# Top-k attention and MLP mixer on one core: score matmuls in chunks of 256 keys, PV over full rows, and a new order

## The chip, the cores and the metric

The kernel runs on one core of a Trainium2 chip. The metric is the device time of one execution in microseconds. The kernel before was timed three times: median 919.33 us, 917.88 to 922.02. The profile comes from one more execution (915.43 us), whose span from the first to the last instruction is 913.6 us.

## What is computed

The attention has 8 batches, 8 heads, 576 positions and a head size of 64; of each row of scores only the 32 largest take part. Its output feeds a mixer MLP over tokens and then over channels.

```python
scores = scale * np.matmul(q, k.transpose(0, 1, 3, 2))          # 8 x 8 x 576 x 576
kth = np.partition(scores, -32, axis=-1)[..., -32:-31]
scores = np.where(scores >= kth, scores, -1e9)
attn = softmax(scores)
x = matmul(attn, v) as [8, 576, 512]
h = relu(x.T @ w_tok1) @ w_tok2                                 # tokens: 576 -> 256 -> 576
u = x + h.T
out = u + relu(u @ w_ch1) @ w_ch2                               # channels: 512 -> 1536 -> 512
```

## The kernel before

**Tiling.** Two heads form a pair, and there are 32 pairs, four to a batch. Keys and queries of a pair are transposed on TensorE, so that head 0 lies on partitions 0 to 63 and head 1 on 64 to 127 of `qT` and `kT`. The 576 queries are cut into five groups `g` of 128; the fifth has 64 queries of each head, and both heads share one tile in it. So a pair has nine rows of work, called heads here: two for each of the groups 0 to 3, and one for group 4.

**A unit of work** is one group of a pair (`unit_ops`, line 419). TensorE computes the scores into PSUM tiles `big`, one for each head, in fp32, which takes two passes per matmul in the trace (`scores`, line 355; L367 for groups 0 to 3, L358 for group 4). ScalarE copies them to `S` (L424). VectorE finds the maxima in seven segments (L431), reduces them (L434, L435, L442) to a first threshold `thi`. ScalarE compares (L445), GpSimd, called POOL in the profile, builds `X` (L448), and VectorE takes from it the 32nd largest value `tlo` (L460). With that threshold the probabilities `Pm` are made in one of several forms:

- D: ScalarE takes the exponential, POOL builds a mask and multiplies (L470 to L479).
- R: ScalarE builds `M`, which is zero for a kept score (L486). TensorE computes the scores a second time and adds `M` times a large negative diagonal, `sink`, to them in PSUM (L504 to L509). ScalarE's exponential of the sum is zero where the sink went in (L512). Q is like R with POOL building `M`.
- A: ScalarE takes the exponential into PSUM, and VectorE compares and multiplies in one instruction (L520).

`FORMS` (line 25) gives the form of each group, one string for even pairs and one for odd ones.

**PV.** A DMA transposes `Pm` into `PT`, ten blocks of 128 x 128, five blocks of keys for each head. `Pm` has 640 columns, of which the last 64 are zeros, written once at the start. `pv` (line 383, matmuls at L390) then multiplies the blocks with `vb`, the values with a column of ones behind them, 65 columns. The fifth block holds only 64 keys, and the kernel before lets that matmul run on 64 rows (`kr`). A pair has 5 groups x 2 heads x 5 blocks = 50 matmuls. VectorE normalises (`norm`, L408 and L409) into `Xb`.

**MLP.** After four pairs of a batch, `mlp_ops` (line 549) runs the mixer: L574 and L579, L595 to L602, L617, L635 and L640 on TensorE, with ScalarE's evictions at L608, L623 and L648.

**The order.** Each piece of work is entered in a `Plan` (line 46) with its engine, an expected duration in us, a due time, what it depends on, and which buffers it takes and frees. `Plan.run` is a list scheduler: on each engine it takes the piece that can start first, and of nearly equal ones the one that is due first. The instructions are issued in the order that comes out, and each engine works through its own in that fixed order. The due times are `W` (line 19) times `T`. So the numbers in `plan.add(...)` and `W` decide no arithmetic, only the order. The four PSUM tiles `big`[...] are the scarcest buffers: scores, transposes, PV, the repeated scores, form A's exponential and the MLP all take theirs from them.

At the end VectorE checks counts and thresholds, and a branch (from line 852) recomputes everything exactly if the check fires; with these inputs it isn't taken.

Of the kernel before, what the change touches and what calls it, by code (L numbers as in the profile page):

```python
# [8 lines left out]
P = 128  # L9
# [7 lines left out]
SINK2 = float(2.0**50)  # L17

W = dict(
    T=2.75, ev=1.35, evh=0.6, seg=0.35, t2=1.2, ct=4.85, xm=3.0, dm=2.3, m5=3.05, ex=3.45, tn=2.3,  # L20
    z=5.1, mk=3.65, pm=4.55, rw=3.7, og=4.8, eg=4.5, ea=3.2, st=4.65, tr=1.7, pv=6.0, fin=6.85,
    mlp=8.85, stp=1.45,
)

FORMS = ("DRADD", "RDADR")
NEG = -float(2.0**120)
BIG = float(2.0**60)

# [143 lines left out]
def kernel(  # L172
# [19 lines left out]
    B, H, S, D = q.shape  # L192
# [6 lines left out]
    SM = 512  # L199
    ST = S - SM  # L200
# [15 lines left out]
    plan = Plan()  # L216
# [69 lines left out]
    T = W["T"]  # L286
# [8 lines left out]
    def pair_ops(p):  # L295
        b, h0 = divmod(p, 4)
        h0 *= 2
        t0 = 9 * p * T
        qL, kL, vL, vb = Buf("qL"), Buf("kL"), Buf("vL"), Buf("vb")
        qT, kT = Buf("qT"), Buf("kT")  # L300
        keng = nc.scalar if p == 0 else nc.sync

        def ld_main(buf, src, eng):
            for h in range(2):
                eng.dma_start(
                    out=buf.t[:, 0:4, h, :],
                    in_=src[b, h0 + h, 0:SM, :].rearrange("(p t) d -> p t d", t=4),
                )

        def ld_q():  # L310
            ld_main(qL, q, nc.sync)
            for h in range(2):
                nc.sync.dma_start(
                    out=qL.t[64 * h : 64 * h + ST, 4, h, :], in_=q[b, h0 + h, SM:S, :]
                )

        def ld_kv(buf, src, eng):
            def f():
                ld_main(buf, src, eng)
                eng.dma_start(  # L320
                    out=buf.t[0:ST, 4, :, :],
                    in_=src[b, h0 : h0 + 2, SM:S, :].rearrange("h p d -> p h d"),
                )
            return f

        tl = t0 - 12 * T
        lq = plan.add("SP", 0.24, tl, ld_q, acq=[qL], dma=1.4)
        lk = plan.add("SP", 0.2, tl + 0.1, ld_kv(kL, k, keng), acq=[kL], dma=1.4)
        lv = plan.add("SP", 0.2, tl + 0.2 if p else 4 * T, ld_kv(vL, v, nc.sync), acq=[vL], dma=1.4)

        pq, pk = Buf("big"), Buf("big")

        def tr(dst, src, n):
            def f():
                o = flat(dst.t)
                for t in range(n):
                    nc.tensor.transpose(o[:, t * P : (t + 1) * P], src.t[:, t, :, :], identF[:, :])
                if n == 4:
                    nc.tensor.transpose(o[:, SM:S], src.t[0:ST, 4, :, :], identF[0:ST, 0:ST])
            return f  # L340

        tt = t0 - W["tr"] * T
        oq = plan.add("PE", 0.6, tt, tr(pq, qL, 5), [lq], acq=[pq, qT], use=[qL])
        ok = plan.add("PE", 0.6, tt + 0.5 * T, tr(pk, kL, 4), [lk], acq=[pk, kT], use=[kL])

        def cp(dst, src, n):
            return lambda: nc.scalar.activation(  # L347
                out=dst.t[:, 0:n], in_=flat(src.t)[:, 0:n], func=AF.Copy, scale=HUP)

        eq = plan.add("ACT", 0.6, tt + T, cp(qT, pq, 5 * P), [oq], use=[pq, qT])  # L350
        ek = plan.add("ACT", 0.57, tt + 1.5 * T, cp(kT, pk, S), [ok], use=[pk, kT])
        ov = plan.add("ACT", 0.6, t0 + 4 * T, lambda: nc.scalar.copy(
            out=vb.t[:, :, :, 0:D], in_=vL.t[:, :, :, :]), [lv], acq=[vb], use=[vL])

        def scores(g, bs, stop):
            if g == 4:
                for lo, hi in ((0, SM), (SM, S)):
                    nc.tensor.matmul(  # L358
                        out=flat(bs[0].t)[:, lo:hi], lhsT=qT.t[:, SM : SM + P], rhs=kT.t[:, lo:hi],
                        start=True, stop=stop,  # L360
                    )
                return

            for lo, hi in ((0, SM), (SM, S)):
                for h in range(2):
                    r = slice(64 * h, 64 * h + 64)
                    nc.tensor.matmul(  # L367
                        out=flat(bs[h].t)[:, lo:hi], lhsT=qT.t[r, g * P : (g + 1) * P],
                        rhs=kT.t[r, lo:hi], start=True, stop=stop,
                    )  # L370

        PT = []
        for g in range(5):
            n = 2 if g < 4 else 1
            bs, Ss = [Buf("big") for _ in range(n)], Buf("S")
            i0 = 9 * p + 2 * g
            om = plan.add("PE", 1.05, T * i0, lambda g=g, bs=bs: scores(g, bs, True), [eq, ek], acq=bs + [Ss], use=[qT, kT])
            PT.append(unit_ops(i0, n, bs, Ss, om, p, g, scores, [qT, kT]))


        O, rd = Buf("big"), Buf("rd")

        def pv(gs):
            for g in gs:
                src = PT[g][0].t
                for h in range(2):
                    o = O.t[:, h, 0 : 5 * (D + 1)].rearrange("p (t d) -> p t d", t=5)
                    for j in range(5):
                        kr = P if j < 4 else ST
                        nc.tensor.matmul(  # L390
                            out=o[:, g, :], lhsT=src[0:kr, (5 * h if g < 4 else 0) + j, :],
                            rhs=vb.t[0:kr, j, h, :], start=(j == 0), stop=(j == 4),
                        )

        if b not in xb:
            xb[b] = Buf("Xb")
        X = xb[b]
        tv = t0 + (9 + W["pv"]) * T
        o = None
        for gs in ((range(5),) if p < NPAIR - 1 else ((0, 1), (2,), (3,), (4,))):  # L400
            o = plan.add("PE", 0.44 * len(gs), tv + gs[0], lambda gs=gs: pv(gs), [PT[g][1] for g in gs] + [ov, o],
                         acq=([] if o else [O] + ([X] if X.users == 0 else [])),
                         use=[PT[g][0] for g in gs] + [vb, X, O])


        def norm():
            o = O.t[:, :, 0 : 5 * (D + 1)].rearrange("p h (t d) -> p h t d", t=5)
            nc.vector.reciprocal(rd.t[:, :, :], o[:, :, :, D])  # L408
            nc.vector.tensor_tensor(  # L409
                out=X.t[:, :, h0 * D : (h0 + 2) * D].rearrange("p t (h d) -> p h t d", h=2),  # L410
                in0=o[:, :, :, 0:D], in1=rd.t[:, :, :].unsqueeze(3).to_broadcast([P, 2, 5, D]), op=ALU.mult,
            )

        nm = plan.add("DVE", 0.86, tv + T, norm, [o], acq=[rd], use=[O, X])
        mixed.setdefault(b, []).append(nm)
# [3 lines left out]
    def unit_ops(i0, n, s, S_, om, p, g, scores, qkT):  # L419

        sg, X, Pm, PT = Buf("sg"), Buf("X"), Buf("Pm"), Buf("PT")
# [60 lines left out]
        elif form in ("R", "Q"):  # L482
# [18 lines left out]
                    op1=ALU.max), zs, acq=[Wm], use=[Z])]  # L501

            def again():
                scores(g, es, False)  # L504
                for h in range(n):
                    for lo, hi in ((0, SM), (SM, S)):
                        nc.tensor.matmul(  # L507
                            out=flat(es[h].t)[:, lo:hi], lhsT=sink[:, "RQ".index(form), :], rhs=Wm.t[:, h, lo:hi],
                            start=False, stop=True)  # L509

            og = plan.add("PE", 1.05 + 0.25 * n, te + W["og"] * T, again, ws, acq=es, use=[Wm] + qkT)
            last = [plan.add("ACT", 0.535, te + W["eg"] * T + 0.2 * h, lambda h=h: nc.scalar.activation(  # L512
                out=Pm.t[:, h, 0:S], in_=flat(es[h].t)[:, 0:S], func=AF.Exp, scale=scale / UP),
                [og], acq=[Pm] if h == 0 else [], use=[es[h], Pm]) for h in range(n)]
# [34 lines left out]
    def mlp_ops(b):  # L549
        X = xb[b]  # L550
        fin = b == B - 1
# [59 lines left out]
        for fc in range(NF):  # L611
            pb = Buf("big")

            def f(fc=fc, pb=pb):
                for lo, hi in ((0, SM), (SM, S)):
                    for cc in range(NC):
                        nc.tensor.matmul(  # L617
                            out=flat(pb.t)[:, lo:hi], lhsT=wc1b[:, cc, fc * P : (fc + 1) * P],
                            rhs=UT.t[:, cc, lo:hi], start=(cc == 0), stop=(cc == NC - 1))

            d = due()
            o = plan.add("PE", 1.05, d, f, uts + l3, acq=[pb] + ([H2] if fc == 0 else []), use=[UT, H2])
            h2.append(plan.add("ACT", 0.535, d + 1, lambda fc=fc, pb=pb: nc.scalar.activation(  # L623
                out=H2.t[:, fc, :], in_=flat(pb.t)[:, 0:S], func=AF.Relu), [o], use=[pb, H2]))
        for s0 in (0, 2, 4):
# [4 lines left out]
            for h in range(sn):  # L630
                for part in range(2):
                    def f(part=part, sc=s0 + h, h=h, pb=pb, r=r):
# [5 lines left out]
                        if part:  # L638
                            for cc in range(NC):
# [2 lines left out]
                                    start=False, stop=(cc == NC - 1))  # L642

                    d = due()
                    o = plan.add("PE", 1.55 if part else 1.3, d, f, dep + l4,
                                 acq=[pb, ob] if (h, part) == (0, 0) else [], use=[H2, pb] + ([UT] if part else []))
                    dep = [o]
            e = plan.add("ACT", 0.1 + 0.4 * sn, d + 1, lambda pb=pb, ob=ob, r=r, sn=sn: nc.scalar.copy(  # L648
# [255 lines left out]
```

## Time and profile before

| | us or share |
|---|---|
| time, median of 3 | 919.33 |
| span of the profiled execution | 913.6 |
| TensorE busy (PE) | 809.9, 89% |
| VectorE busy (DVE) | 794.2, 87% |
| ScalarE busy (ACT) | 757.1, 83% |
| GpSimd busy (POOL) | 722.3, 79% |
| score matmuls L367, busy | 269.9 |
| PV matmuls L390, busy | 125.6 |
| mean granted TensorE clock | 0.885 |

Busy is the union of an engine's instructions in time, so matmuls that overlap count once. PEld is the loading of weights, which runs beside the matmuls. PEclk in a view is the share of full clock that the chip granted TensorE in that stretch: 1.00 is full speed and 0.50 half. In the lists of groups, a line gives the source line, the engine, the operation, output and inputs, the shapes and the count; then busy us and the mean ns of one, and behind the second bar the idle time ahead of the group with what ended it. In the list of waits, a line reads: who waited, for whom, us in total, times, the longest in us.

### The profile page before, as it was taken

To read this page: it belongs to the slowest core of one execution; us is meant where nothing else is said; L and a number is where in the kernel's file an instruction comes from. 1 tells how busy PE (TensorE), PEld (TensorE's weight loads), DVE (VectorE), ACT (ScalarE), POOL (GpSimd) and SP (SyncE) were. 2 spreads that over 40 slices of the span, in tenths; PEclk is the share of its full clock that TensorE was granted. 3 is DMA by queue.
4 is the path that set the end of the run, shared out by engine and by line. 5 is a ranking of instruction groups with operands and counts; after the bars stand their busy time and mean duration, and the time that the engine had idled before them with its cause. 6 is when DMAs were issued, how large, how long until landed. Compare 5 with 4: busy or idle time off the path is not lost.

```text
span 913.6 us, 19343 instructions
## 1 busy us (share of the span) xinstructions
PE 809.9 (89%) x5411; PEld 465.4 (51%) x5411; DVE 794.2 (87%) x4780; ACT 757.1 (83%) x1428; POOL 722.3 (79%) x557
## 2 busy tenths in 40 slices
PE   7778788989899989999789988899799998899996
PEld 4445544555555545555455554555455544455553
DVE  5988999989999999989998998899899889997630
ACT  6876979878999989979889888898898788996641
POOL 2888898879888989869878888888788798886800
PEclk9655769989899999989789997999899898997888
DMA  5965664454654555354544464544563535332501
GB/s 129 155 110 110 112 119 90 77 103 97 139 83 99 128 125 106 73 112 104 104 87 90 98 130 100 83 93 111 107 124 65 116 84 110 66 66 44 108 10 56
DMA packets 311028, 89.57 MB, mean 98 GB/s; under 512 B 303744, under 2 KB 305664, under 8 KB 310912
## 3 DMA queue, kind: packets, MB, share of 16 engines
q1 hardware_dynamic: 306960, 84.19, 45.8%
q0 software_dynamic: 2752, 3.77, 2.9%
q8 instruction: 44, 0.72, 0.3%
q14 instruction: 72, 0.59, 0.2%
q10 hardware_dynamic: 1200, 0.30, 0.1%
HBM read 35.85 MB, written 9.44 MB: 50 GB/s over the span
## 4 chain that ended last, share of the span: by engine, by line
PE 53%; DVE 24%; ACT 13%; POOL 4%; issue 3%; DMA 2%; SPq 1%; DVEq 0%; ACTq 0%; POOLq 0%
PE big L367 15%; PE big L390 12%; PE big L635 11%; DVE cd L431 9%; PE big L617 6%; DVE tlo L460 5%; ACT sg L445 4%; ACT S L424 3%; PE big L507 3%; DVE cd L435 3%; PE big L358 2%; DVE Pm L520 2%; ACT M L486 2%; DVE Xb L409 1%; DVE m L434 1%
## 5 line engine op out<-in xcount | busy, mean ns | idle before, releaser
L431 DVE MAX8 cd<-S 128x8 f32<-128x82 f32 (+1 forms) x2016 | 404.6, 231 | 23.6 <-ACT S L424 23.4
L448 POOL TENSOR_TENSOR X<-S,sg 128x1152 f32<-128x1152 f32 (+1 forms) x160 | 343.0, 2159 | 60.4 <-ACT sg L445 57.8
L367 PE MATMUL big<-kT,qT 64*128 64x512 f32 (+1 forms) x1288 | 269.9, 523 | 32.4 <-ACT kT L347 18.6
L445 ACT ACTIVATE sg<-S,thi 128x576 bf16<-128x576 f32 x288 | 225.6, 785 | 23.5 <-DVE thi L442 19.4
L367 PEld LDWEIGHTS big<-kT,qT 64*128 64x128 f32 x1288 | 149.1, 223 | 153.9 <-issue 95.4
L460 DVE MAX8 tlo<-X 128x8 f32<-128x588 f32 x288 | 220.5, 766 | 5.4 <-POOL X L448 4.8
L424 ACT COPY S<-big 128x576 f32<-128x576 f32 x288 | 175.0, 644 | 42.0 <-PE big L367 34.7
L479 POOL TENSOR_TENSOR Pm<-E,M 128x1152 bf16<-128x1152 bf16 (+1 forms) x79 | 169.6, 2147 | 6.3
L390 PE MATMUL big<-vb,PT 128*128 128x65 bf16 (+1 forms) x1600 | 125.6, 205 | 8.7 <-ACT H L623 4.0
L617 PE MATMUL big<-UT,wc1b 128*128 128x512 bf16 (+1 forms) x768 | 111.7, 298 | 17.8 <-ACT S L424 11.8
L473 POOL TENSOR_SCALAR Z<-S,nt 128x576 f32<-128x576 f32 x142 | 106.2, 748 | 13.4
L635 PE MATMUL big<-wc2b,H 128*128 128x512 bf16 (+1 forms) x480 | 113.8, 381 | 1.3 <-DVE Pm L520 0.8
L390 PEld LDWEIGHTS <-PT 128*128 128x128 bf16 (+1 forms) x1600 | 91.1, 100 | 44.2 <-issue 7.8
L434 DVE MAX8 m<-cd 128x8 f32<-128x14 f32 (+1 forms) x576 | 97.5, 170 | 0.6
L435 DVE MATCH_REPLACE8 cd<-m,cd 128x14 f32<-128x14 f32 (+1 forms) x576 | 97.5, 170 | 0.0
L617 PEld LDWEIGHTS <-wc1b 128*128 128x128 bf16 x768 | 54.9, 101 | 72.9 <-issue 29.0
L476 POOL TENSOR_SCALAR M<-Z 128x1152 bf16<-128x1152 f32 (+1 forms) x79 | 83.0, 1050 | 6.8
L468 ACT ACTIVATE E<-S 128x1152 bf16<-128x1152 f32 (+1 forms) x79 | 84.8, 1075 | 1.9 <-POOL Pm L479 0.3
L623 ACT ACTIVATE H<-big 128x576 bf16<-128x576 f32 x96 | 61.9, 665 | 15.5 <-PE big L617 14.9
L635 PEld LDWEIGHTS <-H 128*128 128x128 bf16 (+1 forms) x480 | 44.2, 100 | 47.0 <-issue 1.8
L512 ACT ACTIVATE Pm<-big 128x576 bf16<-128x576 f32 x81 | 48.9, 646 | 23.1 <-PE big L507 22.9
L358 PE MATMUL big<-kT,qT 128*128 128x64 f32 (+1 forms) x188 | 64.4, 467 | 2.6 <-DVE Xb L409 1.4
(78 smaller groups left out, 872.9 us busy)
## 6 DMA issues: line engine op xcount, KB each, us to landing
qL<-in_q_dram SPq DMA_DIRECT2D x64, 128.0 KB, 2.8
vL<-in_v_dram SPq DMA_DIRECT2D x64, 128.0 KB, 2.8
out_dram<-ob SPq DMA_DIRECT2D x16, 512.0 KB, 3.0
kL<-in_k_dram SPq DMA_DIRECT2D x62, 128.0 KB, 2.8
PT<-Pm SPq DMA_TRANSPOSE x158, 3.5
wc1b<-in_moe_w_ch_dram POOLq DMA_DIRECT2D x4, 384.0 KB, 5.6
wc2b<-in_moe_w_ch_dram POOLq DMA_DIRECT2D x4, 384.0 KB, 5.4
qL<-in_q_dram SPq DMA_DIRECT2D x64, 16.0 KB, 2.4
```

The lines of the kernel that those rows point to most:

```text
L367: nc.tensor.matmul(out=flat(bs[h].t)[:, lo:hi], lhsT=qT.t[r, g * P : (g + 1) * P], rhs=kT.t[r, lo:hi], start=True, stop=stop,)
L390: nc.tensor.matmul(out=o[:, g, :], lhsT=src[0:kr, (5 * h if g < 4 else 0) + j, :], rhs=vb.t[0:kr, j, h, :], start=(j == 0), stop=(j == 4),)
L424: evs = [plan.add("ACT", 0.525, t + W["ev"] * T + W["evh"] * h * T, lambda h=h: nc.scalar.copy(out=S_.t[:, h, :], in_=flat(s[h].t)[:, 0:S] ...
L431: segs = [plan.add("DVE", 0.146, th + W["seg"] * T + 0.01 * a, lambda a=a, cd=cd, h=h: nc.vector.max(cd.t[:, a, :], S_.t[:, h, bounds[a] : ...
L434: m_ = lambda n_, cd=cd, m8=m8: (lambda: nc.vector.max(m8.t[:, :], cd.t[:, :, 0:n_]))
L435: c_ = lambda n_, cd=cd, m8=m8: (lambda: nc.vector.match_replace(cd.t[:, :, 0:n_], m8.t[:, :], cd.t[:, :, 0:n_], NEG))
L445: cts.append(plan.add("ACT", 0.77, th + W["ct"] * T, lambda h=h, i=i, r=r: nc.scalar.activation(out=sg.t[:, h, :], in_=S_.t[:, h, :], func ...
L448: xm = plan.add("POOL", 0.12 + 1.11 * n, te + W["xm"] * T, lambda: nc.gpsimd.tensor_tensor(out=X.t[:, XW - S : XW - S + n * S].rearrange(" ...
L460: m = plan.add("DVE", 0.675, te + W["m5"] * T + 0.3 * h * T, lambda h=h, r=r: nc.vector.max(tlo[:, r : r + 8], X.t[:, h * XW : (h + 1) * X ...
L479: last = [plan.add("POOL", 0.12 + 1.11 * n, te + W["pm"] * T, lambda: nc.gpsimd.tensor_tensor(out=Pm.t[:, 0:n, 0:S], in0=E.t[:, 0:n, :], i ...
L617: nc.tensor.matmul(out=flat(pb.t)[:, lo:hi], lhsT=wc1b[:, cc, fc * P : (fc + 1) * P], rhs=UT.t[:, cc, lo:hi], start=(cc == 0), stop=(cc == ...
L635: nc.tensor.matmul(out=pb.t[0:r, h, 0:C], lhsT=H2.t[:, fc, cs], rhs=wc2b[:, fc, :], start=(fc == 0), stop=False)
```

## The change

The score matmuls of groups 0 to 3 are cut from chunks of 512 and 64 keys into 256, 256 and 64, alternating between the heads. Where scores are computed a second time, the sinks now come first and open the accumulation, and the scores add to them. [...]PV's fifth block runs on all 128 rows; rows 64 to 127 of it are zeros. `W`, the durations in the plan and `FORMS` are changed, and with them the order on every engine. The forms of even pairs are the same in number, with A and D of groups 2 and 3 exchanged.

```diff
-    T=2.75, ev=1.35, evh=0.6, seg=0.35, t2=1.2, ct=4.85, xm=3.0, dm=2.3, m5=3.05, ex=3.45, tn=2.3,
-    z=5.1, mk=3.65, pm=4.55, rw=3.7, og=4.8, eg=4.5, ea=3.2, st=4.65, tr=1.7, pv=6.0, fin=6.85,
-    mlp=8.85, stp=1.45,
+    T=2.45, ev=1.35, evh=1.4, seg=1.35, t2=1.8, ct=2.8, xm=4.4, dm=3.5, m5=4.2, ex=2.45, tn=2.6,
+    z=6.3, mk=4.95, pm=4.65, rw=3.5, og=5.45, eg=4.9, ea=2.8, st=4.45, tr=3.0, pv=7.2, fin=8.2,
+    mlp=10.95, stp=1.05,
 )
-FORMS = ("DRADD", "RDADR")
+FORMS = ("DRDAD", "RDADR")
...
-        oq = plan.add("PE", 0.6, tt, tr(pq, qL, 5), [lq], acq=[pq, qT], use=[qL])
-        ok = plan.add("PE", 0.6, tt + 0.5 * T, tr(pk, kL, 4), [lk], acq=[pk, kT], use=[kL])
+        oq = plan.add("PE", 0.75, tt, tr(pq, qL, 5), [lq], acq=[pq, qT], use=[qL])
+        ok = plan.add("PE", 0.75, tt + 0.5 * T, tr(pk, kL, 4), [lk], acq=[pk, kT], use=[kL])
...
-        def scores(g, bs, stop):
+        def scores(g, bs, start):
...
-                        start=True, stop=stop,
+                        start=start, stop=True,
...
-            for lo, hi in ((0, SM), (SM, S)):
+            for lo, hi in ((0, SM // 2), (SM // 2, SM), (SM, S)):
...
-                        rhs=kT.t[r, lo:hi], start=True, stop=stop,
+                        rhs=kT.t[r, lo:hi], start=start, stop=start or hi > SM // 2,
...
-            om = plan.add("PE", 1.05, T * i0, lambda g=g, bs=bs: scores(g, bs, True), [eq, ek], acq=bs + [Ss], use=[qT, kT])
+            om = plan.add("PE", 1.25 if g < 4 else 1.1, T * i0, lambda g=g, bs=bs: scores(g, bs, True), [eq, ek], acq=bs + [Ss], use=[qT, kT])
...
-                        kr = P if j < 4 else ST
...
-                            out=o[:, g, :], lhsT=src[0:kr, (5 * h if g < 4 else 0) + j, :],
-                            rhs=vb.t[0:kr, j, h, :], start=(j == 0), stop=(j == 4),
+                            out=o[:, g, :], lhsT=src[:, (5 * h if g < 4 else 0) + j, :],
+                            rhs=vb.t[:, j, h, :], start=(j == 0), stop=(j == 4),
...
-            o = plan.add("PE", 0.44 * len(gs), tv + gs[0], lambda gs=gs: pv(gs), [PT[g][1] for g in gs] + [ov, o],
+            o = plan.add("PE", 0.4 * len(gs), tv + gs[0], lambda gs=gs: pv(gs), [PT[g][1] for g in gs] + [ov, o],
...
             def again():
-                scores(g, es, False)
                 for h in range(n):
                     for lo, hi in ((0, SM), (SM, S)):
                         nc.tensor.matmul(
                             out=flat(es[h].t)[:, lo:hi], lhsT=sink[:, "RQ".index(form), :], rhs=Wm.t[:, h, lo:hi],
-                            start=False, stop=True)
+                            start=True, stop=False)
+                scores(g, es, False)
-            og = plan.add("PE", 1.05 + 0.25 * n, te + W["og"] * T, again, ws, acq=es, use=[Wm] + qkT)
+            og = plan.add("PE", (1.25 if n == 2 else 1.1) + 0.33 * n, te + W["og"] * T, again, ws, acq=es, use=[Wm] + qkT)
...
-            o = plan.add("PE", 1.05, d, f, uts + l3, acq=[pb] + ([H2] if fc == 0 else []), use=[UT, H2])
+            o = plan.add("PE", 1.1, d, f, uts + l3, acq=[pb] + ([H2] if fc == 0 else []), use=[UT, H2])
...
-                    o = plan.add("PE", 1.55 if part else 1.3, d, f, dep + l4,
+                    o = plan.add("PE", 1.6 if part else 1.33, d, f, dep + l4,
```

In the rewritten file the sinks stand at L506; the other lines named here keep their numbers.

## The prediction

> **What bounds the kernel now.** I read the page's part 1 and its clock row first, then the chain that ended last, then the busy times by stretch, then who VectorE waits for, and last the forms of the PV matmuls.
>
> ```profile
> PE 809.9 (89%) x5411; PEld 465.4 (51%) x5411; DVE 794.2 (87%) x4780; ACT 757.1 (83%) x1428; POOL 722.3 (79%) x557
> ...
> PEclk9655769989899999989789997999899898997888
> ...
> PE 53%; DVE 24%; ACT 13%; POOL 4%; issue 3%; DMA 2%; SPq 1%; DVEq 0%; ACTq 0%; POOLq 0%
> PE big L367 15%; PE big L390 12%; PE big L635 11%; DVE cd L431 9%; PE big L617 6%; DVE tlo L460 5%; ACT sg L445 4%; ACT S L424 3%; PE big L507 3%; DVE cd L435 3%; PE big L358 2%; DVE Pm L520 2%; ACT M L486 2%; DVE Xb L409 1%; DVE m L434 1%
> ```
>
> Four engines are nearly full. TensorE leads both in busy time and on the chain, and PV (L390) holds 12% of the chain. Now the span in three stretches, start, middle and tail (columns as the first line names them):
>
> ```profile
> core 0: us, PE busy (x) PEld busy (x) DVE busy (x) ACT busy (x) POOL busy (x), PEclk, DMA share, GB/s
> 0.00:20.00 20.00, 13.19 (x57) 7.80 (x58) 9.54 (x92) 11.77 (x21) 3.04 (x8) 1.00 0.58 131
> 20.00:860.00 840.00, 752.26 (x5041) 433.60 (x5040) 773.52 (x4665) 728.33 (x1382) 715.03 (x549) 0.88 0.51 101
> 860.00:914.00 54.00, 44.41 (x316) 23.99 (x314) 11.09 (x24) 16.97 (x26) 4.26 (x3) 0.85 0.14 36
> ```
>
> In the 840 us of the middle VectorE works 773.52 and stands still for 66.5. So VectorE has the longest work there of all engines, and TensorE's slowness shows as VectorE's waiting. The waits of VectorE in that stretch:
>
> ```profile
> DVE rd L408 <- PE big L390: 36.9, 25, 3.2
> DVE cd L431 <- ACT S L424: 14.3, 13, 3.1
> DVE X L456 <- ACT sg L445: 4.7, 6, 1.5
> DVE Pm L520 <- ACT big L517: 2.8, 7, 0.7
> ```
>
> More than half of its standing still, 36.9 of 66.5 us, is the normalisation (L408) at the head of its queue waiting for PV: 25 times of 32, 1.5 us each. PV is what this change touches. Its forms (busy us, mean ns | idle before):
>
> ```profile
> L390 PE MATMUL big<-vb,PT 128*128 128x65 bf16 x1280 | 100.4, 204 | 8.7 <-ACT H L623 4.0 <-ACT S L424 2.6 <-DMA PT<-Pm 2.1
> L390 PE MATMUL big<-vb,PT 64*128 64x65 bf16 x320 | 66.1, 206 | 0.0
> ```
>
> The 320 matmuls on 64 rows are a fifth of PV, yet occupy 66.1 us beside 100.4 for the other four fifths. The single records say why: in the pass at 427.8 us full-row matmuls start 36 ns apart, the 64-row one 125 ns after its predecessor, and the next full-row one 133 ns after that. Medians over the trace at full clock: 36, 125 and 133 ns. A group of five thus takes 3 x 36 + 125 + 133 = 366 ns, and a pair's ten groups 3.66 us; the trace has 3.5 to 3.7.
>
> The last reading is the clock around that pass:
>
> ```profile
> 424.30:427.70 3.40, 3.40 (x26) 1.90 (x26) 3.40 (x21) 3.40 (x7) 3.03 (x5) 1.00 0.14 26
> 427.70:431.10 3.40, 3.40 (x52) 2.50 (x51) 1.44 (x6) 3.14 (x7) 3.32 (x3) 1.00 0.54 110
> 431.10:434.50 3.40, 3.40 (x15) 1.90 (x15) 3.10 (x16) 1.63 (x3) 3.40 (x2) 0.50 0.39 83
> ```
>
> The second row is nothing but PV, TensorE busy throughout, and VectorE works 1.44 of 3.40 us. Then the granted clock falls to 0.50 for a window. Of the 30 half-clock stretches in the trace (211 us in all), 16 (102 us) follow a window of which PV fills half or more.
>
> [...]here the first fp32 pass of a score matmul shows 534 ns to the next pass where later ones show 427, a difference of 107.[...]
>
> **The change part by part.**
>
> *PV on full rows.* Same 1600 matmuls[...]. A group goes from 366 to 5 x 36 = 180 ns, a pair from 3.66 to 1.8, plus 0.1 for the entry: 1.9 us. The extra rows are zeros and cost no columns. Over 32 pairs that is 32 x 1.75 = 56 us of TensorE at full clock. Bounds: 29 ns a matmul (the 64-column matmuls of L617 run at that) gives 1.45 us a pair, and 53 ns (the half-clock spacing) gives 2.65.
>
> *The clock.* A PV of 1.9 us fills half a window[...]. I take two thirds of the 102 us behind PV back to full clock; at half clock TensorE loses half, so some 34 us of its work. Bounds: none, and 51 us. TensorE then has about 810 - 56 - 34 = 720 us of work.
>
> *Score chunks of 256.* 322 matmuls of 512 columns become 644 of 256, each in two fp32 passes. The heads already run side by side: in the unit at 407.9 us the first passes of both start 7 ns apart. A 512 pass takes 427 ns, so a 256 pass takes 213; the next weight load (182 to 190 ns at full clock, 330 beside a pass of 427 at half) starts with the pass before and hides behind it. I take nothing. Upper bound: the two added passes per pair of heads each expose a load of 107 to 187 ns, 161 units x 2, or 34 to 60 us of TensorE.
>
> *Sinks before scores.* Same matmuls. TensorE waited 19.1 us in 9 waits (L507 for M) with the repeated scores already done; now the scores, 1.2 us, come behind that wait: up to 9 x 1.2 = 11 us of TensorE, and behind them whatever is queued, mostly the next first scores, for which ScalarE's eviction (L424) and then VectorE's maxima wait. I take 5 us of TensorE, hidden by its new slack.
>
> *Orders.* The planner charged PV 2.2 us where the trace has 3.6, and scores 1.05 where a unit takes 1.23; its normalisations stand where PV should be finished, hence the 25 waits. The new charges (PV 2.0, scores 1.25) sit beside what I expect (1.9 and 1.23). Counting instructions, TensorE has issued on average 2.6 heads more than VectorE has begun when PV meets its normalisation, against 2.15 before, in a pattern that repeats every four pairs. The counts of the D, R and A forms are unchanged (FORMS only permutes them), so VectorE's 794 us of work stay.
>
> *Sum.* VectorE becomes the bound. Of its PV waits I keep a quarter, 9 us (passes that still meet half clock); of the other 29.6 us of idle, 24. The middle is then 773.5 + 9 + 24 = 806.5. Start 20; the tail has two shares of a PV, 54 - 3 = 51. Span 877.5; the timed runs stand 919.3 - 913.6 = 5.7 above the profiled span, of which I take 3.5: 881 us.
>
> **The rivals.**
> 1. *VectorE runs almost without a gap.* If the half-clock stretches mostly vanish, its middle idle falls to 12 us: 20 + 785.5 + 50 + 3.5 = 859. For: 300 to 400 us reached 95.67 of 100 even with PV waits. Against: ScalarE and POOL are over 83% full at that pace.
> 2. *A wait takes the place of the PV wait* (L431 for L424, L460 for POOL's X): 50 us of idle stay, 20 + 823.5 + 51 + 3.5 = 898. For: ScalarE and POOL have 728 and 715 us in the middle. Against: neither is what VectorE mostly waits for now.
> 3. *The chunks cost what PV saves.* Exposed loads of 60 us and stalls of 11 at the sinks eat 56: TensorE stays the bound, the half clock remains, and the new order gives nothing: 920 to 935, say 926. Against: loads shorter than the passes.
>
> **How the numbers follow.** Forecast 0.66, rival 1 0.12, rival 2 0.15, rival 3 0.07. Range 855 to 907: it holds the forecast with its bounds, rival 1 and most of rival 2, and leaves out rival 3. Faster by over 0.5% (below 914.7): all but rival 3 and a corner of rival 2, 0.91. Within: 0.03. Slower: 0.06.
>
> **What would show it.** L390 busy near 60 us rather than 125.6, no 64-row form; the wait L408 for L390 under 12 us; mean clock above 0.90; TensorE's share on the chain below VectorE's; L367 with passes near 213 ns apart. Wrong if L390's spacing stays above 50 ns, if L367's busy time grows by 30 us or more, or if VectorE's idle time in the middle stays above 50 us under another name.

## The result and the profile after

The changed kernel takes 850.74 us (845.87 to 851.52), beside 920.67 us for the kernel before on the same chip. The ratio is 0.9235, with a 95% interval from 0.9187 to 0.9282. The forecast was 881 with a range from 855 to 907: the direction was right, and the gain of 70 us is nearly twice what was forecast and beyond the range.

From the page of the changed kernel, the busy times, the clock row and the chain (the shares add up to 53% of the span; the rest of it this chain does not put down to anyone):

```profile
PE 695.2 (82%) x6055; PEld 473.5 (56%) x6055; DVE 788.7 (93%) x4780; ACT 754.4 (89%) x1428; POOL 722.5 (86%) x557
...
PEclk8686669999899999999999999999999999999998
...
DVE 29%; POOL 11%; PE 9%; ACT 3%; issue 1%; POOLq 0%; ACTq 0%; DVEq 0%
```

TensorE went from 810 to 695 us of busy time and from first to third on the chain. VectorE is now the fullest engine, at 93%. From the seventh of its 40 slices on, the clock row stands at 9 but for two 8s. The same three stretches as before, with borders moved to the shorter span:

```profile
core 0: us, PE busy (x) PEld busy (x) DVE busy (x) ACT busy (x) POOL busy (x), PEclk, DMA share, GB/s
0.00:20.00 20.00, 12.17 (x62) 9.10 (x63) 9.75 (x93) 11.88 (x21) 2.96 (x7) 0.90 0.57 129
20.00:800.00 780.00, 649.27 (x5709) 445.67 (x5708) 767.98 (x4666) 727.45 (x1386) 718.29 (x551) 0.93 0.57 109
800.00:845.00 45.00, 33.73 (x287) 18.75 (x285) 10.95 (x24) 15.06 (x24) 1.20 (x1) 0.93 0.14 39
```

In the middle VectorE works 767.98 of 780 us. It stands still for 12 us, where it was 66.5. What it waits for there:

```profile
DVE cd L431 <- ACT S L424: 3.2, 4, 1.5
DVE rd L408 <- PE big L390: 3.1, 4, 1.5
DVE tlo L460 <- POOL X L448: 1.3, 2, 1.1
```

The wait for PV fell from 36.9 to 3.1 us, and the wait for ScalarE's evictions from 14.3 to 3.2 along with it. And the forms of PV, sinks and scores (busy us, mean ns | idle before):

```profile
L367 PE MATMUL big<-kT,qT 64*128 64x256 f32 x1288 | 209.9, 432 | 22.2 <-ACT kT L347 12.2 <-ACT S L424 7.3 <-DVE Xb L409 2.2
...
L390 PE MATMUL big<-vb,PT 128*128 128x65 bf16 x1600 | 58.3, 197 | 7.2 <-DMA PT<-Pm 6.1 <-ACT H L623 1.1
L506 PE MATMUL big<-M,sink 128*128 128x512 bf16 x81 | 29.7, 404 | 52.4 <-ACT M L486 43.1 <-ACT S L424 5.1 <-ACT H L623 3.4
```

PV occupies 58.3 us in one form where it took 125.6 in two. The sinks now wait longer than before: 43.1 us for M, against 19.1.

### The profile page after: what moved, and what is told of

Same layout as the page of the kernel before. It is cut to its first block, busy times and chain, and to the rows that moved or that the text cites. A ratio compares the mean times of both kernels' runs of the same rounds, so it can differ in the third digit from the quotient of the medians.

```text
span 844.1 us, 20557 instructions
## 1 busy us (share of the span) xinstructions
PE 695.2 (82%) x6055; PEld 473.5 (56%) x6055; DVE 788.7 (93%) x4780; ACT 754.4 (89%) x1428; POOL 722.5 (86%) x557
## 4 chain that ended last, share of the span: by engine, by line
DVE 29%; POOL 11%; PE 9%; ACT 3%; issue 1%; POOLq 0%; ACTq 0%; DVEq 0%
DVE cd L431 10%; DVE tlo L460 7%; POOL X L448 5%; PE big L635 3%; DVE cd L435 3%; POOL Pm L479 3%; PE big L617 2%; DVE Pm L520 2%; DVE m L434 2%; POOL Z L473 2%; PE big L367 2%; DVE Xb L409 2%; POOL M L476 1%; DVE X L456 1%; DVE thi L442 1%
## 5 line engine op out<-in xcount | busy, mean ns | idle before, releaser
L431 DVE MAX8 cd<-S 128x8 f32<-128x82 f32 (+1 forms) x2016 | 409.4, 231 | 12.1 <-ACT S L424 12.1
L448 POOL TENSOR_TENSOR X<-S,sg 128x1152 f32<-128x1152 f32 (+1 forms) x160 | 343.8, 2165 | 29.6 <-ACT sg L445 28.6
L367 PE MATMUL big<-kT,qT 64*128 64x256 f32 (+1 forms) x1932 | 233.2, 373 | 22.2 <-ACT kT L347 12.2
L367 PEld LDWEIGHTS big<-kT,qT 64*128 64x128 f32 x1932 | 193.0, 202 | 62.9 <-ACT kT L347 13.6
L460 DVE MAX8 tlo<-X 128x8 f32<-128x588 f32 x288 | 220.2, 764 | 2.5 <-POOL X L448 1.3
L424 ACT COPY S<-big 128x576 f32<-128x576 f32 x288 | 177.3, 648 | 13.2 <-PE big L367 10.8
L617 PE MATMUL big<-UT,wc1b 128*128 128x512 bf16 (+1 forms) x768 | 107.0, 290 | 26.9 <-ACT Pm L512 12.3
L617 PEld LDWEIGHTS <-wc1b 128*128 128x128 bf16 x768 | 55.3, 99 | 78.2 <-issue 31.1
L434 DVE MAX8 m<-cd 128x8 f32<-128x14 f32 x576 | 98.3, 171 | 0.5
L435 DVE MATCH_REPLACE8 cd<-m,cd 128x14 f32<-128x14 f32 x576 | 98.0, 170 | 0.0
L506 PE MATMUL big<-M,sink 128*128 128x512 bf16 (+1 forms) x162 | 31.6, 302 | 52.4 <-ACT M L486 43.1
L358 PE MATMUL big<-kT,qT 128*128 128x64 f32 (+1 forms) x188 | 67.3, 486 | 6.0 <-ACT S L424 4.2
L390 PE MATMUL big<-vb,PT 128*128 128x65 bf16 x1600 | 58.3, 197 | 7.2 <-DMA PT<-Pm 6.1
L486 ACT ACTIVATE M<-S,tlo 128x576 bf16<-128x576 f32 x81 | 60.7, 785 | 2.7 <-DVE tlo L460 2.3
```

What stands on the lines that cost most here:

```text
L367: nc.tensor.matmul(out=flat(bs[h].t)[:, lo:hi], lhsT=qT.t[r, g * P : (g + 1) * P], rhs=kT.t[r, lo:hi], start=start, stop=start or hi > SM ...
L424: evs = [plan.add("ACT", 0.525, t + W["ev"] * T + W["evh"] * h * T, lambda h=h: nc.scalar.copy(out=S_.t[:, h, :], in_=flat(s[h].t)[:, 0:S] ...
L431: segs = [plan.add("DVE", 0.146, th + W["seg"] * T + 0.01 * a, lambda a=a, cd=cd, h=h: nc.vector.max(cd.t[:, a, :], S_.t[:, h, bounds[a] : ...
L434: m_ = lambda n_, cd=cd, m8=m8: (lambda: nc.vector.max(m8.t[:, :], cd.t[:, :, 0:n_]))
L435: c_ = lambda n_, cd=cd, m8=m8: (lambda: nc.vector.match_replace(cd.t[:, :, 0:n_], m8.t[:, :], cd.t[:, :, 0:n_], NEG))
L448: xm = plan.add("POOL", 0.12 + 1.11 * n, te + W["xm"] * T, lambda: nc.gpsimd.tensor_tensor(out=X.t[:, XW - S : XW - S + n * S].rearrange(" ...
```

## The experiments

In what follows the span of each trace is cut into four parts: the start up to VectorE's first maximum (L431), its work from there to the last `tlo` (L460), its idle time between the two, and the tail from there to the end. They add up to the span. "PV wait" is the idle time of the normalisation (L408), whatever ended it. "Half clock" is the sum of the stretches in which the clock record shows 0.5. All are worked out from the single records of each trace. The parts are of the one profiled execution of each kernel, and the time is the median of its timed executions.

The clock record goes in steps of 3.41 us: each half-clock stretch in the traces of before and after lasts 3.41 us or a multiple of it, but for the last one of each. A window is 3.41 us of the record. "Mixed PV" is PV as it was before, with a matmul on 64 rows behind every four on 128. In its trace the two starts around a step from 128 to 64 rows stand 125 ns apart and those around the step back 133, where full-row matmuls stand 36 apart (medians at full clock). The expectations call such a step a change of mode and the longer gap a drain; what TensorE does in the gap is not shown.

| run | time us | ratio to before, interval | start | work | idle | tail | PV wait | half clock |
|---|---|---|---|---|---|---|---|---|
| before | 920.7 | 1 | 12.2 | 784.3 | 72.4 | 44.6 | 41.1 | 211.5 |
| after | 850.7 | 0.9235 (0.9187-0.9282) | 11.2 | 779.6 | 12.9 | 40.4 | 3.7 | 113.5 |
| pv_alone | 859.7 | 0.9343 (0.9308-0.9378) | 11.6 | 781.5 | 20.2 | 40.9 | 3.8 | 136.6 |
| order_alone | 880.9 | 0.9566 (0.9539-0.9592) | 11.1 | 780.5 | 40.8 | 45.0 | 31.7 | 153.5 |
| pv_undone | 877.6 | 0.9516 (0.9480-0.9551) | 11.5 | 780.8 | 41.0 | 43.6 | 30.3 | 142.3 |
| chunks_undone | 850.4 | 0.9218 (0.9193-0.9243) | 11.5 | 779.9 | 17.5 | 40.3 | 7.0 | 111.1 |
| pv_twice | 876.0 | 0.9524 (0.9495-0.9554) | 11.8 | 782.1 | 35.2 | 41.6 | 24.9 | 114.8 |
| pv_twice_new | 864.9 | 0.9400 (0.9380-0.9420) | 11.5 | 780.5 | 27.7 | 41.5 | 18.6 | 95.8 |
| pv_charge | 893.5 | 0.9699 (0.9668-0.9730) | 11.6 | 785.5 | 49.8 | 46.0 | 13.3 | 202.3 |
| pv_grouped | 863.3 | 0.9391 (0.9345-0.9436) | 12.2 | 781.4 | 22.2 | 43.7 | 6.2 | 143.8 |
| chunks_alone | 926.9 | 1.0081 (1.0056-1.0107) | 12.5 | 785.5 | 86.4 | 41.9 | 50.4 | 220.6 |
| after_side | 850.1 | 0.9253 (0.9222-0.9284) | 12.0 | 779.9 | 15.6 | 40.4 | 4.6 | 122.1 |
| sinks_last_side | 845.0 | 0.9200 (0.9172-0.9228) | 11.9 | 779.4 | 11.3 | 40.2 | 1.8 | 113.9 |
| forms_8 | 865.3 | 0.9385 (0.9350-0.9421) | 10.9 | 779.9 | 31.8 | 40.8 | 8.5 | 119.7 |
| dummies_pool | 904.6 | 0.9806 (0.9767-0.9846) | 11.3 | 790.9 | 51.1 | 49.5 | 5.2 | 148.2 |

Start and work move little, the tail by up to 9 us, and above all the time follows the idle column. So the question of each run is what fills or empties VectorE's idle time.

### PV on full rows alone

```diff
-                        kr = P if j < 4 else ST
...
-                            out=o[:, g, :], lhsT=src[0:kr, (5 * h if g < 4 else 0) + j, :],
-                            rhs=vb.t[0:kr, j, h, :], start=(j == 0), stop=(j == 4),
+                            out=o[:, g, :], lhsT=src[:, (5 * h if g < 4 else 0) + j, :],
+                            rhs=vb.t[:, j, h, :], start=(j == 0), stop=(j == 4),
```

> The kernel before with PV's fifth block on full rows, all else and the order as before. Theory P (the drains and the half clock behind them made TensorE late, and VectorE stood still for it): most of the 70 us comes back, 860 to 880 us, L390 busy near 60 us, L408's wait for L390 under 12 us, and VectorE's other waits shrink too, without any new order. Theory O (the new order closes VectorE's gaps): 890 to 905, with L424's and POOL's waits as before.

859.7 us: 62.6 us below the 922.3 of the kernel before on the same chip, with no new order. The idle time falls from 72.4 to 20.2. VectorE's waits of this run, between 20 and 800 us:

```profile
DVE cd L431 <- ACT S L424: 5.1, 6, 1.9
DVE rd L408 <- PE big L390: 3.2, 4, 1.6
DVE tlo L460 <- POOL X L448: 1.4, 5, 0.5
```

The waits for ScalarE shrank as well: those for the evictions (L424) from 14.3 to 5.1, and all that bear ScalarE's name from 24.8 (20 to 860 us of the kernel before) to 6.1. Nothing of ScalarE's was changed, so these were TensorE's lateness handed on: a late score is evicted late. The wait for POOL's X was small before, 1.7 us, and is 1.4. Outside the PV wait, the idle time of the table fell from 31.3 to 16.4 us. The time comes out just under theory P's 860 to 880.

### The new order alone, and PV undone in the changed kernel

Both put PV back on 64 rows in the fifth block. `order_alone` also has the chunks and the sinks of before, so it differs from the kernel before only in `W`, `FORMS` and the plan's durations.

> The kernel before with the new W, FORMS and durations, so the new order, but PV on 64 rows in the fifth block, chunks of 512 and the sinks last. Theory P: 895 to 920, the PV waits stay over 25 us and half-clock stretches still follow PV. Theory O: 865 to 885.

> The changed kernel with PV's fifth block on 64 rows again. Theory P: 895 to 920. Theory O: 865 to 880. If the two parts add up, this time less the changed kernel's is the time of before less pv_alone's.

The order alone brings 41 us, and with PV undone the changed kernel still stands 44.6 us below before. That is more than theory P allowed, and both times lie within theory O. But the two gains don't add: 62.6 + 41.4 would be 104, and together they are 70. Both empty the same idle time, and no run of this study brings it below 11 us. What stays in order_alone, here between 20 and 835 us, is mostly PV, as theory P had it:

```profile
DVE rd L408 <- PE big L390: 24.2, 21, 3.4
DVE rd L408 <- ACT H L623: 5.9, 5, 1.3
DVE cd L431 <- ACT S L424: 4.3, 4, 1.5
```

21 of 32 normalisations wait for PV, against 25 in the kernel before, for 1.2 us each. The new order has shrunk the rest: outside the PV wait 9.1 us of idle time are left of 31.3, fewer than the 16.4 of pv_alone. It also does better by the clock: 6 half-clock stretches follow a window that PV fills by half or more, where there were 16, though PV is as long as before.

### One number of the plan

```diff
-            o = plan.add("PE", 0.44 * len(gs), tv + gs[0], lambda gs=gs: pv(gs), [PT[g][1] for g in gs] + [ov, o],
+            o = plan.add("PE", 0.73 * len(gs), tv + gs[0], lambda gs=gs: pv(gs), [PT[g][1] for g in gs] + [ov, o],
```

> The kernel before with one number changed: the plan charges PV 0.73 us a group instead of 0.44, what the drained PV takes, so normalisations and all that follows are placed later. If the wrong charge made VectorE wait: L408's wait for L390 falls from 37 us below 12 and the time to 880 to 895. If TensorE's lateness is spread over everything and only its name is PV: the wait falls but others grow, 905 to 922.

893.5 us, 27 below before, with the instructions of before in another order and the clock no better (202 us at half, 0.888 mean). The PV wait fell to 13.3, not quite below the 12 of the first theory, and the time lies in its range. But the wait of L431 for L424, over the whole trace, rose from 23.4 to 32.8, as the second has it. So a charge 1.4 us too low for each PV cost real time. The PV wait fell by 28 us, as much as the time; but the charge moves all that follows, so that the place of the normalisation alone did it is not shown. A true charge doesn't give TensorE its time back.

### Length or clock

```diff
-                    for j in range(5):
+                    for j in (0, 1, 2, 3, 4, 0, 1, 2, 3, 4):
```

This runs each full-row group twice, in the order of before (pv_twice) and in the changed kernel (pv_twice_new).

> The kernel before, in its order, with PV on full rows and each group of five matmuls run twice, the second time over the first. A pair's PV then takes 100 x 36 ns, 3.6 us, as long as the drained one[...]. Theory 'time' (PV's length alone made TensorE late): 900 to 922 us. Theory 'clock' (the half clock behind the drains did it): 865 to 880, no half-clock stretch behind PV, mean clock 0.92 or more. A share between: 880 to 900.

> The changed kernel with each PV group run twice on full rows: as long as with the drain, without its half clock. The run with the drain put back took 877.6 us. Theory 'time': 870 to 880 again. Theory 'clock': 850 to 860.

In the old order, 876.0: of the 61 us that full rows bring, 45 come although PV is nearly as long as mixed PV. A doubled PV takes 3.2 us at full clock from its first start to its last end, where mixed PV takes 3.7, because its matmuls start 29 ns apart (median) and not 36 as forecast. So a few of the 45 us are still length: halving PV from here brought 16 us for 1.5 us a pair, so 0.5 us a pair is worth some 5, an estimate. So roughly 40 of the 61 us go with the clock, an estimate too. The clock record bears it out. A window of nearly pure doubled PV and the window behind it (columns as above):

```profile
512.20:515.60 3.40, 3.06 (x101) 2.94 (x97) 2.13 (x8) 3.40 (x6) 3.05 (x5) 1.00 0.10 37
515.60:519.00 3.40, 1.97 (x11) 1.31 (x12) 3.38 (x22) 2.26 (x5) 3.32 (x3) 1.00 0.68 202
```

101 matmuls in 3.40 us, and the clock stays at 1.00. The mixed PV of the kernel before got 52 into such a window, at a higher busy share of TensorE (3.40 against 3.06), and the clock fell to 0.50 behind it. Over the whole traces: of 32 full-clock windows that mixed PV filled by half or more, 16 were followed by half clock; of 31 such windows in pv_twice, none. The mean busy share of TensorE in these windows is the same in both, 0.90. The last section estimates what differs.

In the new order the run lies between the two theories, at 864.9: by the ratios, 11 of the 26 us between pv_undone and after come with full rows at nearly the old length and 15 with the shorter PV.

### Is it the 64 rows, or the change between?

```diff
-            for g in gs:
...
-                    for j in range(5):
+            for js in ((0, 1, 2, 3), (4,)):
+                for g in gs:
...
+                        for j in js:
...
-                            rhs=vb.t[0:kr, j, h, :], start=(j == 0), stop=(j == 4),
+                                rhs=vb.t[0:kr, j, h, :], start=(j == 0 and g == gs[0]), stop=(j == 4 and g == gs[-1]),
```

> The kernel before, in its order, with the 64-row matmuls of a pair's PV gathered behind its forty full-row ones, so two changes of mode for a pair instead of twenty; the number of 64-row matmuls, their rows and the plan stay. If the change of mode costs (theory P): a pair's PV takes 50 x 36 ns and two drains, some 2.0 us, and the time comes out as with full rows, 855 to 866. If a 64-row matmul is slow by itself: 3.0 us or more a pair, and 885 or more.

863.3 us, with all 320 matmuls still on 64 rows. The forms of this trace, where PV is at L391:

```profile
L391 PE MATMUL big<-vb,PT 128*128 128x65 bf16 x1280 | 50.1, 200 | 17.1 <-DMA PT<-Pm 10.8 <-ACT H L624 3.9 <-ACT S L425 2.3
L391 PE MATMUL big<-vb,PT 64*128 64x65 bf16 x320 | 16.7, 196 | 0.0
```

The 64-row form went from 66.1 to 16.7 us without losing a matmul. Between starts, medians at full clock: 29 ns from full to full, 33 from 64 to 64, and 128 from full to 64. What costs here is the step from 128 to 64 rows, 128 ns; the shape doesn't, at 33 against 29. Nor is it the border between two accumulation groups, which in the kernel before falls on the same place: in pv_alone that border is still there behind every fifth matmul, and the starts across it are 29 ns apart (median at full clock).

### Chunks and sinks

chunks_undone keeps the sinks first. chunks_alone puts both into the kernel before. sinks_last has chunks of 512 and the scores ahead of the sinks, with all else of the changed kernel.

```diff
-            for lo, hi in ((0, SM // 2), (SM // 2, SM), (SM, S)):
+            for lo, hi in ((0, SM), (SM, S)):
...
             def again():
+                scores(g, es, False)
...
-                            start=True, stop=False)
-                scores(g, es, False)
+                            start=False, stop=True)
```

> The changed kernel with score chunks of 512 and 64, sinks first. As forecast, the chunks cost and bring nothing: 847 to 855. The rival, that chunks of 256 are worth something of their own (the two heads run side by side more often): 858 or more. If they cost weight loads: under 845.

> The kernel before, in its order, with chunks of 256 and the sinks first, PV left on 64 rows. TensorE is late here, so a cost of the chunks would show: if they cost nothing and the sinks 5 us of TensorE, 918 to 928; if the chunks expose weight loads, 940 or more; if they help by themselves, under 912.

> The changed kernel with chunks of 512 and the scores ahead of the sinks, as before; PV on full rows and the new order stay. If scores behind the wait for M cost something, this is the faster one, 840 to 847. If TensorE's slack hides it, 848 to 854.

The chunks do nothing: 850.4 against 850.7 us. In a unit at full clock a head's passes of 256 start 216 ns apart (320 behind the first, with its load), and a unit takes 1.302 us with chunks of 256 and 1.297 with 512 (medians, first start to last end), so no weight load shows as lost time and none is won.

Sinks and chunks together cost the kernel before 7 us, with an interval clear of 1. The waits of TensorE show where, the first line from the kernel before, the second from this run:

```profile
PE big L507 <- ACT M L486: 19.1, 9, 4.0
PE big L506 <- ACT M L486: 39.9, 15, 6.1
```

The matmul that waits for M now stands ahead of the scores instead of behind them, so the scores can't fill the wait. sinks_last came out at 846.7 us (ratio 0.9198, 0.9164 to 0.9233), 4 us under the changed kernel, but not measured beside it. The two side by side:

> The changed kernel itself, beside the next one on the same chip, 848 to 853.

> Chunks of 512 and scores ahead of the sinks, with PV on full rows and the new order. If the sinks' place and the chunks cost the changed kernel something, 3 to 6 us under it with intervals that part; if its 846.7 was chance, within 2 us of it.

850.1 and 845.0 us. The six times of one, 847.4 to 852.1, and of the other, 843.8 to 846.5, don't overlap, though the two intervals against before overlap a little, at 0.922. The wait for M shows the difference. TensorE's longest wait in the trace of after_side:

```profile
PE big L506 <- ACT M L486: 43.9, 15, 11.2
```

The same in the trace of sinks_last_side, where the sinks stand at L507:

```profile
PE big L507 <- ACT M L486: 23.2, 13, 6.7
```

Since the chunks cost nothing, the 5 us belong to the place of the sinks. This version, with chunks of 512, sinks last, PV on full rows and the new order, is the fastest of the study.

That chunks of 256 need the sinks ahead of the scores was not shown: no run has such chunks with the sinks last. pv_grouped speaks against it. In all pairs but the last it has a single `start` for the five accumulation groups of a head, on the first of them, and accumulates correctly in all five. The second chunk of 256 might open in this way, without a `start`, and leave the sinks last.

### Two tries to relieve VectorE

```diff
-FORMS = ("DRDAD", "RDADR")
+FORMS = ("DRDAD", "RDADR", "DRDAD", "RDRDR")
```

```diff
-            dm = plan.add("DVE", 0.125, te + W["dm"] * T, lambda h=h, i=i: nc.vector.tensor_scalar(
+            onp = form_of(p, g) != "D"
+            dm = plan.add("POOL" if onp else "DVE", 0.17 if onp else 0.125, te + W["dm"] * T, lambda h=h, i=i, e=(nc.gpsimd if onp else nc.vector): e.tensor_scalar(
```

> The changed kernel with form R in place of A in every fourth pair (7 units of two heads). If VectorE's work is now the bound: it loses 14 x 0.72 = 10 us of work, ScalarE gains about 11 and TensorE 13, and the time falls by 5 to 10 us, to 841 to 846. If ScalarE is as much the bound: 849 to 858.

> The changed kernel with the small fill of X (L456) on POOL instead of VectorE for the units of forms R and A, 146 of 288 heads. VectorE loses 146 x 0.125 = 18 us, POOL gains about 28 us, to 750 us. If VectorE's work is the bound: 830 to 840. If POOL's or a shared wait takes over: 848 to 860.

Both missed: 865.3 and 904.6 us, slower than the changed kernel. They took work from VectorE, but its busy time did not fall (779.9 and 790.9 against 779.6), and its idle time rose to 31.8 and 51.1. In dummies_pool 19 us of the idle time are waits for POOL by the maximum that gives `tlo` (11.0 for the fill, 7.7 for X): the fill takes 277 ns on POOL against 208 on VectorE, and it queues among instructions of 2 us. The waits for ScalarE's evictions (L431 for L424) grew by 14 us more, from 12.1 to 26.5.

Why the busy time holds can be read from the records. Successive instructions of VectorE overlap, and busy time counts an overlap once. The durations added up did fall, by 13 us in forms_8 and 28 in dummies_pool, but the overlap fell as much. L435 needs the maximum of L434: where it comes directly behind it, it starts 210 ns later, while a maximum of another head (L431) starts 95 ns behind L434. The changed kernel has 10 such direct pairs, forms_8 51 and dummies_pool 95, and other pairs within one head's chain grow alike (L435 ahead of L434 or L442). So part of VectorE's waiting is hidden in its busy time, wherever the order leaves it nothing to put between. `W` was not refitted to either, so they don't show that VectorE's work can't be reduced with gain.

## Why the prediction was right and wrong

**What bounds the kernel** was right: VectorE's idle time is what the change moves, and PV was the name on most of it. After the change VectorE is the bound, with 98.5% of the middle.

**PV on full rows**: right in kind, and a little better than forecast. A group starts its matmuls 29 ns apart instead of 36, a pair takes 1.7 us at full clock from first start to last end, and L390 58.3 us in all ("near 60").

**The clock**: right in kind and too small. Two thirds of the 102 us behind PV were to come back, 68 us; the half-clock time fell by 98. A PV of 1.7 us can no longer fill half of a window, but of 18 windows that it fills by 40% or more none is followed by half clock, and of the 18 half-clock stretches left, one follows a window with any PV in it. TensorE's work came to 695 us instead of 720. By pv_twice this part alone is worth some 40 us in the old order, the estimate above. The forecast had it as 34 us of TensorE's work and gave it no term of its own in the sum.

**The sum, where it failed.** The step is "of the other 29.6 us of idle, 24": the waits that bear other names than PV were kept almost whole, without a reason, as if they were ScalarE's and POOL's own. Measured, 9 us stayed. Both halves of the change shrink them: of the 31.3 us outside the PV wait in the table, PV on full rows alone leaves 16.4, with no change to ScalarE, POOL or the order, and the new order alone leaves 9.1, with mixed PV. They were the lateness of TensorE and the place of the work, not the other engines' speed. This is 15 us of the 30 between 881 and 850.7, the largest single term. The quarter of the PV waits, 9 us, was 3 (6 more). VectorE's work in the middle was 768.0 instead of 773.5 (5.5). The tail was 44 instead of 51 (7): its two shares of PV went from 1.5 and 2.2 us to 0.8 and 1.3, and the 96 matmuls of L617 from 13.75 to 12.07, because the tail no longer enters them at half clock (before, the clock stood at 0.50 from 874.9 to 881.7 us, and they began at 878.0). The addition for the timed runs was 6.6 instead of 3.5, the other way by 3.

**Score chunks**: right, nothing. The bound of 34 to 60 us didn't come up.

**Sinks first**: mis-sized, and that the chunks need it was not shown. TensorE's wait for M grew by 24 us (19.1 to 43.1) where 5 were taken. And the new slack hides only part: side by side it costs 5 us of time.

**Orders**: right that a normalisation placed for a PV of 2.2 us costs time (pv_charge, 27 us from that one number). Not foreseen was that the order alone is worth 41 us even with mixed PV left in: the forecast let it act on the PV waits only. In the sum the two causes overlap, so the order, with chunks and sinks, adds about 9 us to what PV on full rows does (859.7 to 850.7, on two chips).

**The rivals**: rival 1, the one with gapless VectorE, was what happened, and it was sized with the same 12 us of idle that came out. That the size fits so well is luck in part: nothing in the prediction derives the 12 us. It had a chance of 0.12 and stood at 859, because it kept 785.5 and 50 for work with idle and tail where 780 and 44 came. "ScalarE and POOL are over 83% full" spoke against it, but at 89 and 86% they make VectorE wait under 6 us in the middle.

## What to carry to other kernels

When four engines are nearly full, a wait under another engine's name may still be the slow engine's lateness handed on; free the slow one and see before counting those waits as fixed. A short matmul at the end of an accumulation that runs on fewer rows than its neighbours was worth padding with zeros here (62.6 us in pv_alone), or gathering with others like it: the steps before and behind it took 125 and 133 ns, where matmuls of one kind start 29 to 36 ns apart. Charge a static scheduler the measured duration, and put what has to wait behind what need not, not ahead of it.

## What the runs showed of the hardware

A window of TensorE that the profile shows as busy throughout can still be followed by half clock. Of the 32 full-clock windows that mixed PV filled by half or more in the kernel before, 12 had TensorE busy for 91% or less, and all 12 were followed by half clock; of the 20 with 97% or more, 4 were. The doubled PV on full rows was followed by half clock in none of 31 windows, though TensorE stood idle for a part of 13. Over all full-clock windows of the kernel before, of the 130 with TensorE busy for 97% or more 4 were followed by half clock, of the 19 with 50 to 70% 8, so the busy share alone doesn't part them.

What differs between the two kinds of PV can be estimated from the spacings in the traces. At full clock bf16 matmuls of 512 columns start 216 ns apart (L617), so 65 columns account for 27 ns. In the doubled PV that is 27 of the 29 ns from start to start, over nine tenths; in mixed PV it is 5 x 27 = 137 of the 366 ns of a group, 0.37. That the clock goes with this share is an estimate of the author's, which no run was made to test. What decides the clock the traces don't show.

At a step between 128 and 64 rows the starts stand 125 and 133 ns apart in the kernel before, and 128 from full to 64 in pv_grouped. Within a run of one kind they stand 29 to 36 ns apart, 29 and 36 for full rows and 33 for 64. The rows themselves show no cost in the scores before: fp32 passes of 512 columns start 429 ns apart on 64 rows (L367, the unit at 407.9 us) and on 128 (L358, median). At half clock the 512-column matmuls of L617 start 426 ns apart instead of 216, and the full-row ones of mixed PV 53 instead of 36.
